# Attention and channel mix on one core: q and k turned on VectorE instead of TensorE, scores as 32-row matmuls, the mix as scaled copies and a sum

## The chip, the core and the metric

The kernel runs on one core of a Trainium2 chip. The engines are called as in the profile: PE (TensorE), DVE (VectorE), ACT (ScalarE), POOL (GpSimd, here mostly the issuer of loads) and SP (SyncE, the issuer of the other DMAs). The metric is the device time of one execution in microseconds (us).

## What is computed

Eight batches of sliding-window attention with eight heads feed a channel mix (two dense layers and a gate).

```python
def _attn_ref(q, k, v):                      # each 8 x 8 heads x 576 x 64
    scores = scale * np.matmul(q, k.transpose(0, 1, 3, 2))
    bias = slopes[:, None, None] * (-np.abs(rel).astype(np.float32))[None, :, :]
    mask = (rel >= 0) & (rel < window)       # window = 128
    scores = np.where(mask, scores + bias[None], -1000000000.0)
...
    return np.matmul(attn, v)                # attn: softmax of the scores

def _moe_ref(x, mu_k, mu_r, w_k, w_v, w_r):  # x: 8 x 576 x 512
    x_prev = np.concatenate([np.zeros((B, 1, D)), x[:, :-1, :]], axis=1)
    xk = mu_k * x + (1.0 - mu_k) * x_prev
    xr = mu_r * x + (1.0 - mu_r) * x_prev
    k = np.maximum(xk @ w_k, 0.0)
    v = k * k @ w_v
    r = 1.0 / (1.0 + np.exp(-(xr @ w_r)))
    return r * v
```

## The kernel before

**Pairs.** The attention runs in 32 pairs of heads (`it` = 4 b + g: batch b, heads 2g and 2g+1). A batch has 576 tokens: four key blocks of 128 (`NF`) and a tail of 64. Because of the window, key block u meets only the queries of blocks u and u+1, 256 columns.

**Getting q and k head by head in columns.** POOL loads q and k of half a batch, cast to bf16, into `ql` so that partition p holds tokens 4p to 4p+3 (L107); the 64 tail tokens go to `ts` (L101). For each pair DVE reorders q and k by token into `ct` (`by_token`, L126), PE turns them in eight 128x128 transposes into PSUM (`qk_transp`, L135), and ACT copies them to `qk` (`qk_copy`, L115). The tails of a batch take four PE transposes (L148) and two DVE copies (L154, L155).

**Scores and softmax.** `scores(it, e)` (L187) makes one half of a pair's scores in a PSUM buffer `sa`: matmuls of 64 rows (a head's 64 elements), head 0 on partitions 0 to 63, head 1 on 64 to 127. A pair has two halves with six matmuls each, of 256, 128 or 64 columns. There are two `sa` buffers; each half takes one. ACT does the exponential (L195) into `at`, DVE multiplies it with the mask (L200; batch 0 adds the distances on PE instead, L176), PE multiplies with v (L218, again into an `sa` buffer from batch 1 on; a column of ones gives the sum), DVE divides (L229, L230), PE transposes the result (L238) and ACT copies it to `xt` (L243).

**Mix and layers.** For each pair DVE forms `dl` = x - x_prev (L263) and then xk = dl mu_k + x_prev and xr = dl mu_r + x_prev (L270). Two batches together (P) go through the layers: `m1` (L281, xk times w_k, in column ranges of 256, 384 or 512), relu on ACT (L287), its square on DVE (L292), `m2a` and `m2` (L315, times w_v), `m3` (L300, xr times w_r), a tanh on ACT (L306) and the product on DVE (L321), which SP stores (L324).

**Order.** Every engine has a hand-written list, `ORDER`, that fixes the order of its work: `tq` the transposes of q and k, `pq` the copies to `qk`, `score`, `exp`, `mask`, `av` (attention times v), `norm`, `ot` and `xt` (transposed result and its copy), `xk`, `xr`, `m1`, `rl` (relu), `kk` (square), `m2a`, `m2`, `m3`, `rs` (tanh), `oo` (product), `lql`, `lts`, `lvs`, `lwk` (loads). A function `plan` emits the instructions in these orders. Each engine runs its list strictly from first to last. A store is issued with its product; SP has no list of its own.

Of the kernel before, what the change touches and what calls it, by code (L numbers as in the profile page):

```python
# [16 lines left out]
def kernel(  # L17
# [12 lines left out]
    nc = tc.nc  # L30
# [17 lines left out]
    NAT = 4  # L48
    NEARLY = G
    XMUL = ()  # L50
# [4 lines left out]
    csp = ctx.enter_context(tc.tile_pool(name="csp", bufs=3))  # L55
    xup = ctx.enter_context(tc.tile_pool(name="xup", bufs=3))
    mxp = ctx.enter_context(tc.tile_pool(name="mxp", bufs=2))
# [4 lines left out]
    p_tp = ctx.enter_context(tc.tile_pool(name="p_tp", bufs=1, space=bass.MemoryType.PSUM))  # L62
    p_mm = ctx.enter_context(tc.tile_pool(name="p_mm", bufs=3, space=bass.MemoryType.PSUM))
# [4 lines left out]
    ldr = cst.tile([128, 2, NHW, 2, NF * D], FP32, name="ldr")  # L68
    qk_buf = [cst.tile([128, 2, SM], BF16, name=f"qk{i}") for i in range(NBUF)]
    vs_buf = [cst.tile([128, NF, H, W], BF16, name=f"vs{i}") for i in range(NLD)]  # L70
    ql_buf = [cst.tile([128, 2, 2, H // 2, NF * D], BF16, name=f"ql{i}") for i in range(2)]
    ts_buf = [cst.tile([128, H, D], BF16, name=f"ts{i}") for i in range(NLD)]
    at_buf = [cst.tile([128, 2 * 1024 + 64], BF16, name=f"at{i}") for i in range(NAT)]

    tt_buf = [cst.tile([128, G, 3, 64], BF16, name=f"tt{i}") for i in range(2)]
    tv_buf = [cst.tile([128, H, W], BF16, name=f"tv{i}") for i in range(NLD)]
    xt_buf = [cst.tile([128, NPO, 2 + S], BF16, name=f"xt{i}") for i in range(2)]
# [22 lines left out]
    def load_tail(b, i):  # L100
        nc.gpsimd.dma_start(  # L101
            out=ts_buf[b % NLD][64 * i:64 * i + 64],
            in_=(q, k)[i][b, :, SM:S, :].rearrange("h p d -> p h d"))
# [13 lines left out]
    def cast_qk(g, i, f):  # L117
        if i == 0:
            T["cs", g] = csp.tile([128, 2, NF, 2, D], BF16, tag="ct", name="cs")
        f(T["cs", g][:, i].rearrange("p r h d -> p h r d"),  # L120
          ldr[:, i, g].rearrange("p h (r d) -> p h r d", d=D))

    def by_token(it):
        b, g = divmod(it, G)
        T["cs", it] = csp.tile([128, 2, NF, 2, D], BF16, tag="ct", name="ct")
# [18 lines left out]
    def tail_transp(b):  # L144
        ts = ts_buf[b % NLD]
# [6 lines left out]
    def tail_copy(b):  # L152
        t4 = T.pop(("tt", b))[:, 0:128 * G].rearrange("p (g t c) -> p g t c", g=G, t=2)
        nc.vector.tensor_copy(out=tt_buf[b % 2][:, :, 2], in_=t4[:, :, 0])  # L154
        nc.vector.tensor_copy(out=tt_buf[b % 2][:, :, 0], in_=t4[:, :, 1])  # L155
# [10 lines left out]
    def scores(it, e):  # L166
        early = it < NEARLY
        b, g = divmod(it, G)
        qk, tt = qk_buf[it % NBUF], tt_buf[b % 2]
# [19 lines left out]

    def at_half(it, e):  # L190
# [3 lines left out]
    def expo(it, e):  # L194
        nc.scalar.activation(out=at_half(it, e), in_=T.pop(("sa", it, e)),  # L195
                             func=AF.Exp, scale=float(scale))
# [26 lines left out]
    def norm(it, t0, t1):  # L223
# [3 lines left out]
        if t0 == 0 or it < G:  # L227
            xu = T["xu", it, t0] = xup.tile([128, NJ, 2, D], BF16, tag="xu", name="xu")
# [5 lines left out]
    def x_transp(it, t0=0, t1=NJ):  # L234
        xu = T.pop(("xu", it, t0))
        tp = T["xt", it, 128 * t0] = p_tp.tile([128, 1024], BF16, tag="tp", name="tp")
# [4 lines left out]
    def x_copy(it, c0=0, c1=S):  # L241
        b, g = divmod(it, G)
        nc.scalar.copy(out=xt_buf[b % 2][:, g, 2 + c0:2 + c1], in_=T.pop(("xt", it, c0))[:, c0:c1])  # L243

    def x_scaled(it, c0, c1):
        if c0 == 0:
            T["xm", it] = mxp.tile([128, S], BF16, tag="xm", name="xm", bufs=3)
        nc.scalar.activation(out=T["xm", it][:, c0:c1], in_=xt_buf[0][:, it, 2 + c0:2 + c1],
                             func=AF.Identity, scale=mu_sb[:, it:it + 1])

    def mix(it, which, c0=0, c1=S):
        b, g = divmod(it, G)
        P, e = divmod(b, 2)
        xc, xp = xt_buf[b % 2][:, g, 2 + c0:2 + c1], xt_buf[b % 2][:, g, 1 + c0:1 + c1]
        scaled = it in XMUL
        if which == 0:
            if e == 0 and g == 0 and c0 == 0:
                T["xk", P] = mxp.tile([128, NPO, SP], BF16, tag="xk", name="xk")
                T["xr", P] = mxp.tile([128, NPO, SP], BF16, tag="xr", name="xr")
        if c0 == 0 and which == int(scaled):  # L260
            T["dl", it] = mxp.tile([128, S], BF16, tag="dl", name="dl", bufs=4)
# [637 lines left out]
```

## Time and profile before

| | us |
|---|---|
| median of three runs (244.85 to 245.68) | 245.48 |
| span of the profiled execution, from its first to its last instruction | 243.3 |
| lies outside the span, by the median | 2.2 |
| PE busy | 232.5 |
| DVE busy | 202.5 |
| ACT busy | 173.6 |
| POOL busy | 77.2 |

The profiled execution has no time of its own beside its span; the runs' median is set against it. In the prediction, a row of the timeline gives the start, the duration, engine, source line, operation, tiles and count; neighbours of one kind are merged. The distance from one start to the next is what an instruction costs its engine in a dense stretch. A row of the groups ends with busy us, mean ns of one instruction, and the idle time before them with what ended it. A row of the stretches gives the length and then PE, PEld (weight loads), DVE, ACT and POOL busy time with counts, the granted PE clock as a share, the share in which DMA engines were busy and GB/s. The columns of the 40 slices are tenths of busy time.

### The profile page before, as it was taken

Reading aid. Unit: us, or ns where it says so; the run is one execution under the profiler, and the core shown is the slowest. Engines: PE = TensorE matmul, PEld = TensorE weight load, DVE = VectorE, ACT = ScalarE, POOL = GpSimd, SP = SyncE. Lnnn points to the kernel's source line nnn. Section 1 sums busy time; section 2 is a strip of 40 time slices with the busy share of each in tenths; the row PEclk is TensorE's granted clock in tenths of the full one; section 3 lists DMA queues with packets and bytes.
Section 4 is the critical chain, followed back from the end, with each engine's and each line's share of the span. In section 5 each row is a group of like instructions: output and inputs, shape, how many; then the busy total and the mean of one; then the engine's idle time right before and its main releaser. Section 6 shows DMA issues by size and latency. Waiting matters only on the chain.

```text
span 243.3 us, 5721 instructions
## 1 busy us (share of the span) xinstructions
PE 232.5 (96%) x2295; PEld 140.1 (58%) x2295; DVE 202.5 (83%) x448; ACT 173.6 (71%) x281; POOL 77.2 (32%) x115
## 2 busy tenths in 40 slices
PE   7499989999999999999999999999999999999993
PEld 2246776657766656557566575565565656545641
DVE  6388999999999999998989989988779876883333
ACT  6378799979999896986977768878854666307700
POOL 8999485486272825100980000000000000000000
PEclk9999999999999999999999999999999999999999
DMA  7999999999997999921999120110201300132023
GB/s 135 160 155 191 158 174 205 167 185 223 193 150 95 153 194 108 167 52 46 96 174 212 51 89 0 46 46 0 86 34 55 132 1 1 46 129 86 0 89 131
DMA packets 70748, 26.86 MB, mean 110 GB/s; under 512 B 47161, under 2 KB 66113, under 8 KB 70721
## 3 DMA queue, kind: packets, MB, share of 16 engines
q0 software_dynamic: 64976, 16.52, 77.3%
q1 hardware_dynamic: 5744, 9.97, 11.3%
q8 instruction: 18, 0.29, 0.5%
q14 instruction: 10, 0.07, 0.1%
HBM read 33.56 MB, written 9.44 MB: 177 GB/s over the span
## 4 chain that ended last, share of the span: by engine, by line
PE 85%; DVE 8%; DMA 3%; POOL 1%; issue 1%; ACT 1%; POOLq 0%; DVEq 0%
PE pv L315 26%; PE ps L281 24%; PE pr L300 13%; PE sa L187 6%; PE sa L218 6%; PE tp L135 5%; PE tp L238 4%; DMA ql<-in_k_dram 3%; DVE xu L230 2%; DVE xk L270 1%; DVE xr L270 1%; DVE ct L126 1%; DVE kk L292 1%; DVE dl L263 1%; PE to L148 1%
## 5 line engine op out<-in xcount | busy, mean ns | idle before, releaser
L195 ACT ACTIVATE at<-sa 128x1024 bf16<-128x1024 f32 x64 | 65.4, 1037 | 12.1 <-PE sa L187 11.9
L281 PE MATMUL ps<-xk,wk_sb 128*128 128x256 bf16 (+2 forms) x416 | 73.2, 314 | 0.6 <-DVE xk L270 0.6
L315 PE MATMUL pv<-wv_sb,kk 128*128 128x512 bf16 x288 | 69.4, 379 | 0.0
L287 ACT ACTIVATE rl<-ps 128x256 bf16<-128x256 f32 (+2 forms) x104 | 46.9, 475 | 20.8 <-PE ps L281 16.6
L281 PEld LDWEIGHTS <-wk_sb 128*128 128x128 bf16 x416 | 38.2, 98 | 21.5 <-issue 1.3
L292 DVE TENSOR_TENSOR kk<-rl 128x256 bf16<-128x256 bf16 (+2 forms) x104 | 32.7, 335 | 12.9 <-ACT rl L287 12.6
L315 PEld LDWEIGHTS <-kk 128*128 128x128 bf16 x288 | 26.7, 98 | 27.5 <-issue 0.8
L115 ACT COPY qk<-tp 128x1024 bf16<-128x1024 bf16 (+1 forms) x32 | 31.0, 969 | 9.1 <-PE tp L135 5.1
L200 DVE TENSOR_TENSOR at<-at,mask 128x1024 bf16<-128x1024 bf16 x56 | 37.3, 683 | 0.0
L300 PE MATMUL pr<-wr_sb,xr 128*128 128x512 bf16 x144 | 36.0, 379 | 0.0
L87 POOL DMA_DIRECT2D vs<-in_v_dram x32 | 28.5, 905 | 22.5 <-PE sa L218 18.0
L321 DVE SCALAR_TENSOR_TENSOR ot<-rs,pv 128x512 f32<-128x512 bf16 x36 | 24.6, 683 | 11.8 <-PE pv L315 11.6
L270 DVE SCALAR_TENSOR_TENSOR xk<-dl,mu_sb,xt 128x576 bf16<-128x576 bf16 (+2 forms) x36 | 27.1, 752 | 1.3
L243 ACT COPY xt<-tp 128x576 bf16<-128x576 bf16 (+2 forms) x36 | 21.3, 591 | 8.8 <-PE tp L238 8.7
L306 ACT ACTIVATE rs<-pr 128x512 bf16<-128x512 f32 x36 | 22.1, 618 | 5.6 <-PE pr L300 5.5
L270 DVE SCALAR_TENSOR_TENSOR xr<-dl,mu_sb,xt 128x576 bf16<-128x576 bf16 x32 | 25.8, 810 | 0.0
L218 PEld LDWEIGHTS <-at 128*128 128x128 bf16 x576 | 21.6, 98 | 4.7 <-ACT at L195 0.3
L230 DVE TENSOR_TENSOR xu<-sa,rc 128x640 bf16<-128x640 f32 x28 | 23.1, 824 | 1.0
L135 PE MATMUL tp<-ident,ct 128*128 128x128 bf16 x248 | 19.0, 219 | 4.0 <-DVE ct L126 4.0
L135 PEld LDWEIGHTS <-ct 128*128 128x128 bf16 x248 | 15.5, 98 | 8.7 <-DVE ct L126 5.1
L300 PEld LDWEIGHTS <-xr 128*128 128x128 bf16 x144 | 13.3, 98 | 12.1
L187 PE MATMUL sa<-qk 64*128 64x256 bf16 (+1 forms) x256 | 19.8, 259 | 0.4 <-ACT at L195 0.3
(63 smaller groups left out, 215.6 us busy)
## 6 DMA issues: line engine op xcount, KB each, us to landing
out_dram<-ot SPq DMA_DIRECT2D x36, 256.0 KB, 2.0
vs<-in_v_dram POOLq DMA_DIRECT2D x32, 128.0 KB, 7.2
ql<-in_q_dram POOLq DMA_DIRECT2D x15, 256.0 KB, 7.7
ql<-in_k_dram POOLq DMA_DIRECT2D x15, 256.0 KB, 8.2
wk_sb<-in_moe_w_k_dram POOLq DMA_DIRECT2D x2, 512.0 KB, 7.9
wv_sb<-in_moe_w_v_dram POOLq DMA_DIRECT2D x2, 512.0 KB, 10.7
ts<-in_q_dram POOLq DMA_DIRECT2D x8, 64.0 KB, 7.3
ts<-in_k_dram POOLq DMA_DIRECT2D x8, 64.0 KB, 6.3
```

Source lines behind the costliest of these rows:

```text
L115: nc.scalar.copy(out=dst, in_=src)
L135: nc.tensor.transpose(tp[:, 128 * (n - NF * t0):128 * (n - NF * t0) + 128], cs[:, n // NF, n % NF].rearrange("p h d -> p (h d)"), ident)
L187: nc.tensor.matmul(sa[:, hl, c0:c0 + n], lhsT=kk_, rhs=qq_, start=not early, stop=True, skip_group_check=True)
L195: nc.scalar.activation(out=at_half(it, e), in_=T.pop(("sa", it, e)), func=AF.Exp, scale=float(scale))
L200: nc.vector.tensor_tensor(out=at_half(it, e), in0=at_half(it, e), in1=mask[:, 2 * g:2 * g + 2, 256 * e:256 * e + 512], op=ALU.mult)
L218: nc.tensor.matmul(pa[:, hl, W * (t - t0):W * (t - t0) + W], lhsT=at[:, lo:lo + 128], rhs=vs[:, u, 2 * g + hl, :] if u < NF else tvb[:, 2 ...
L270: nc.vector.scalar_tensor_tensor(out=to, in0=T["dl", it][:, c0:c1], scalar=mu_sb[:, NPO * which + g:NPO * which + g + 1], in1=xp, op0=ALU. ...
L281: nc.tensor.matmul(ps[:, 0:c1 - c0], lhsT=wk_sb[:, po, 128 * fo:128 * fo + 128], rhs=xk[:, po, c0:c1], start=(po == 0), stop=(po == NPO - 1))
L287: nc.scalar.activation(out=rl[:, 0:c1 - c0], in_=T.pop(("ps", P, c0, fo))[:, 0:c1 - c0], func=AF.Relu, scale=RELU_SCALE)
L292: nc.vector.tensor_tensor(out=T["kk", P, c0][:, fo, 0:c1 - c0], in0=rl[:, 0:c1 - c0], in1=rl[:, 0:c1 - c0], op=ALU.mult)
L300: nc.tensor.matmul(pr, lhsT=T["xr", P][:, po, 128 * c:128 * c + 128], rhs=wr_sb[:, po], start=(po == 0), stop=(po == NPO - 1))
L315: nc.tensor.matmul(pv, lhsT=kk[:, fo, o:o + 128], rhs=wv_sb[:, fo], start=(fo == 0), stop=(fo == NFO - 1))
```

## The change

**q and k of batches 1 to 7.** They no longer go through `ct`, PE and `qk`. `turn` (L176) reads a half batch of q or k in `ql` as four-byte words, each holding two neighbouring bf16 elements, and transposes blocks of 32 partitions by 32 words on DVE. Afterwards partitions 32u to 32u+31 hold block u of 128 tokens, one word of the head on each partition and the two elements of the word beside each other. `turn_tail` (L184) does the same for the tails, on 32 partitions. `shift` (L192) is a DMA on SP within SBUF that puts the queries of block u+1 beside those of block u. Batch 0 goes the old way.

**Scores of batches 1 to 7.** `scores4` (L237, L242) makes all scores of a pair at once in both `sa` buffers: for each head and each of the two elements of a word four matmuls of 32 rows, one on each group of 32 partitions and each into its own bank, then two of 64 columns for the tail. The exponential reads them in another arrangement (L258).

**Mix.** For xk and xr each, two scaled copies (x mu and x (1 - mu), L315) and a sum with one of them shifted by a token (L317).

**Squares.** 67 of the 104 squares of the relu are done on ACT (L341).

**Buffers and orders.** The PSUM pool of the transposes goes to the pool of the layers (four buffers instead of three and one). Buffers of batch 0 lie in memory that is used later. Every list of `ORDER` is new, and SP has one, with shifts (`sh`) and stores (`st`); on POOL `lwk` stands behind the loads of batch 1's q and k.

```diff
-    p_tp = ctx.enter_context(tc.tile_pool(name="p_tp", bufs=1, space=bass.MemoryType.PSUM))
-    p_mm = ctx.enter_context(tc.tile_pool(name="p_mm", bufs=3, space=bass.MemoryType.PSUM))
+    p_mm = ctx.enter_context(tc.tile_pool(name="p_mm", bufs=4, space=bass.MemoryType.PSUM))
...
+    def turn(b, w, i):
+        hs = slice(w * H // 2, (w + 1) * H // 2)
+        dst = words(kt_buf[b % 2], 128)[:, hs] if i else words(q2_buf[b % 2], 256)[:, hs, 0:128]
+        nc.vector.transpose(
+            dst.rearrange("p h (c r) -> p h r c", r=NF),
+            ql_buf[b % 2][:, w, i].rearrange("p h c -> p (h c)").bitcast(FP32).rearrange(
+                "p (h r d) -> p h r d", r=NF, d=32))
+
+    def turn_tail(b, i):
+        dst = (words(kl_buf[b % 2], 128)[96:128, :, 0:64] if i else
+               words(q2_buf[b % 2], 256)[96:128, :, 128:192])
+        nc.vector.transpose(
+            dst.rearrange("p h (c r) -> p h r c", r=2),
+            tl_buf[b % 2][64:96, i].rearrange("p h c -> p (h c)").bitcast(FP32).rearrange(
+                "p (h r d) -> p h r d", r=2, d=32))
+
+    def shift(b, w):
+        hs = slice(w * H // 2, (w + 1) * H // 2)
+        qt = words(q2_buf[b % 2], 256)[:, hs]
+        nc.sync.dma_start(out=qt[0:96, :, 128:256], in_=qt[32:128, :, 0:128])
...
+        for hl in range(2):
+            h = 2 * g + hl
+            for par in range(2):
+                for u in range(NF):
+                    r, n = 32 * u, 256 if u < NF - 1 else 192
+                    nc.tensor.matmul(
+                        T["sa", it, u // 2][:, u % 2, 256 * hl:256 * hl + n],
+                        lhsT=kt[r:r + 32, h, :, par], rhs=qt[r:r + 32, h, 0:n, par],
+                        start=(par == 0), stop=(par == 1), skip_group_check=True)
+            for par in range(2):
+                nc.tensor.matmul(
+                    T["sa", it, 1][:, 1, 256 * hl + 192:256 * hl + 256],
+                    lhsT=kl[96:128, h, :, par], rhs=qt[96:128, h, 128:192, par],
+                    start=(par == 0), stop=(par == 1), skip_group_check=True)
...
-        if which == int(scaled):
-            nc.vector.tensor_tensor(out=T["dl", it][:, c0:c1], in0=xc, in1=xp, op=ALU.subtract)
...
-        nc.vector.scalar_tensor_tensor(
-            out=to, in0=T["dl", it][:, c0:c1],
-            scalar=mu_sb[:, NPO * which + g:NPO * which + g + 1], in1=xp, op0=ALU.mult, op1=ALU.add)
+        for i in range(2):
+            m = NPO * (2 * i + which) + g
+            nc.vector.tensor_scalar(out=mb[:, 1 - i, 2 + c0:2 + c1], in0=xc,
+                                    scalar1=mu_sb[:, m:m + 1], scalar2=None, op0=ALU.mult)
+        nc.vector.tensor_tensor(
+            out=T["xk" if which == 0 else "xr", P][:, g, S * e + c0:S * e + c1],
+            in0=mb[:, 1, 2 + c0:2 + c1], in1=mb[:, 0, 1 + c0:1 + c1], op=ALU.add)
...
+        if (P, c0, fo) in ACT_SQ:
+            nc.scalar.activation(out=out_, in_=in_, func=AF.Square)
...
-            score.5.0 tq.6 m1.0.256.4 m1.0.256.5 m1.0.256.6 av.4 score.5.1 m1.0.256.2 tail.2 ot.4
+            m1.0.256.2 m1.0.256.5 score.6 m1.0.0.7 m1.0.0.2 m1.0.256.6 m1.0.256.7
```

More of the change, by code (lines that the diff above doesn't have):

```diff
@@ L48 @@
     NAT = 4
+    NMB = 4
     NEARLY = G
-    XMUL = ()
     NHW = 1
@@ L242, in x_copy @@
         b, g = divmod(it, G)
[L243 to L249, printed above, removed]
+        nc.scalar.copy(out=xt_buf[b % 2][:, g, c0:c1], in_=T.pop(("xt", it, c0))[:, c0:c1])
     def mix(it, which, c0=0, c1=S):
@@ L514, in add_pair @@
         else:
+            war = ([("score", G * (b - 2) + i) for i in range(G)] if b > 2 else
+                   [("score", i, h) for i in range(G) for h in range(2)] if b == 2 else [])
             if g == 0:
[L516 to L519 removed]
```

477 lines of the change are left out of this document (260 added, 217 removed).

## The prediction

> **What bounds the kernel now.** I read the page's busy shares first, then its 40 slices, then the chain that ended last.
>
> ```profile
> span 243.3 us, 5721 instructions
> ...
> PE 232.5 (96%) x2295; PEld 140.1 (58%) x2295; DVE 202.5 (83%) x448; ACT 173.6 (71%) x281; POOL 77.2 (32%) x115
> ```
> ```profile
> PE   7499989999999999999999999999999999999993
> ...
> PE 85%; DVE 8%; DMA 3%; POOL 1%; issue 1%; ACT 1%; POOLq 0%; DVEq 0%
> ```
>
> PE is busy for 96% of the span, has a 9 in every slice from the eighth to the last but one, and makes up 85% of the chain; DVE's 83% over the whole span may hide a stretch in which it is full too, which is looked at below. The busy number can't price PE's work, since the ends of matmuls are modelled and overlap. I price by distances between starts, from one stretch of PE's timeline:
>
> ```profile
> 100.21 0.44 PE L238 MATMUL tp<-ident,xu 128*128 128x128 bf16 x5
> 100.58 0.34 PE L187 MATMUL sa<-qk 64*128 64x256 bf16 x4
> ...
> 100.82 0.38 PE L187 MATMUL sa<-qk 64*128 64x256 bf16 x4
> 101.13 1.04 PE L281 MATMUL ps<-xk,wk_sb 128*128 128x512 bf16 x4
> 102.00 0.61 PE L135 MATMUL tp<-ident,ct 128*128 128x128 bf16 x8
> 102.45 0.81 PE L300 MATMUL pr<-wr_sb,xr 128*128 128x512 bf16 x3
> ```
>
> Start to start, five transposes and the gap behind them take 0.37 us, and 5 of 56 ns are 0.28: the remaining 0.09 is lost on going into the 64-row score matmuls. The scores of one pair take 100.58 to 101.13, 0.55, of which 0.1 is lost on going out and 0.44 is streaming (0.22 of the last 0.31 for two pairs of 256 columns, 0.11 a pair: the two heads of a pair stream beside each other). The eight q/k transposes take 102.00 to 102.45, 0.45. For the long matmuls the end of the chain gives the price:
>
> ```profile
> 224.95 0.33 PE ps L281 x2
> ...
> 229.17 1.75 PE ps L281 x16
> 230.92 8.65 PE pv L315 x40
> ```
>
> 40 matmuls of 512 columns in 8.65 us: 216 ns each; in the same way 256 columns cost 109 ns (16 in 1.75) and 384 columns 163. The 18 matmuls that multiply attention with v cost 0.54 us a pair before and after.
>
> As a test of these prices I multiplied them with the counts in the hand-written PE order of before: 219.0 us of work, plus 39 entries into score matmuls (31 of them from batch 1 on) at 0.19 us for both switches, is 226.4. The last matmul group ends at 230.92+8.65 = 239.57, so 13.1 us of the span are PE idle, and busy times by stretches say where:
>
> ```profile
> 0.00:40.00 40.00, 32.99 (x395) 21.38 (x396) 31.99 (x96) 29.60 (x53) 32.99 (x59) 1.00 1.70 166
> 40.00:60.00 20.00, 20.00 (x231) 12.25 (x230) 19.72 (x41) 17.31 (x26) 12.46 (x17) 1.00 2.04 193
> 60.00:80.00 20.00, 20.00 (x233) 13.48 (x230) 19.39 (x44) 19.39 (x33) 9.57 (x13) 1.00 1.40 143
> 80.00:100.00 20.00, 20.00 (x219) 11.59 (x217) 19.72 (x42) 16.69 (x24) 10.82 (x14) 1.00 1.44 158
> ```
>
> After 40 us PE (the first busy column) loses nothing, at a granted clock of 1.00; DVE (the third) has 1.2 us free in 60. The 7.0 us free in the first 40, and some waits there that the modelled ends hide, are the 13.1. So PE work taken out after 40 us shortens the run one for one, as long as DVE can follow. That "as long as" is the prediction.
>
> **The change part by part.**
>
> *PE.* Batches 1 to 7 have 28 pairs. Each loses 8 transposes (0.45 us) and a quarter of the four tail transposes of its batch (0.06). The scores become 20 matmuls of 32 rows: per head two passes (even and odd elements of the bf16 pairs) of 256, 256, 256 and 192 columns, one on each group of 32 partitions and each into its own PSUM bank, and two of 64. If the four groups stream beside each other, as the two heads do now, each group carries 512 columns per head, 213 ns, and with starts 3 to 4 ns apart a pair takes 0.46 us against 0.44. Entries fall from 39 to 36. The order of after then sums to 205.3+6.8 = 212.1 us: 14.3 less.
>
> Two things here are shown by no row. Both operands are now read with a step of two elements: a set of four matmuls that streams at half rate takes 0.11 us longer, and a pair has four, so between 0 and 0.44 us a pair, 0 and 12 us in all. And there are four row groups instead of two: between full overlap and none, which is 16 matmuls of 0.1 us and four of 0.03 instead of 0.46, +1.3 us a pair, 36 in all. I take full rate and full overlap, since the nearest rows, with two groups, show both. A gain below 0.44 us is excluded, as each group has the 512 columns per head that it has now.
>
> *DVE.* The prices, again start to start:
>
> ```profile
> 36.96 0.81 DVE L270 SCALAR_TENSOR_TENSOR xr<-dl,mu_sb,xt 128x576 bf16<-128x576 bf16 x1
> 37.69 1.29 DVE L200 TENSOR_TENSOR at<-at,mask 128x1024 bf16<-128x1024 bf16 x2
> 38.89 0.28 DVE L292 TENSOR_TENSOR kk<-rl 128x256 bf16<-128x256 bf16 x1
> 39.10 0.28 DVE L154 COPY tt<-to 128x256 bf16<-128x256 bf16 x1
> ...
> 39.49 0.67 DVE L126 COPY ct<-ql 128x1024 bf16<-128x1024 bf16 x1
> ...
> 41.47 0.45 DVE L263 TENSOR_TENSOR dl<-xt 128x576 bf16<-128x576 bf16 x1
> 41.95 0.82 DVE L270 SCALAR_TENSOR_TENSOR xk<-dl,mu_sb,xt 128x576 bf16<-128x576 bf16 x1
> 42.69 0.69 DVE L200 TENSOR_TENSOR at<-at,mask 128x1024 bf16<-128x1024 bf16 x1
> ...
> 44.09 0.42 DVE L126 COPY ct<-ql 128x1024 bf16<-128x1024 bf16 x1
> 44.43 0.49 DVE L292 TENSOR_TENSOR kk<-rl 128x256 bf16<-128x256 bf16 x2
> ```
>
> xr 0.73, one mask 0.60, the tail copies 0.39, dl and xk together 1.22, ct 0.34, one square of 256 columns 0.20. The duration of a row is 0.08 more than its distance to the next, because neighbours overlap.
>
> ```profile
> L321 DVE SCALAR_TENSOR_TENSOR ot<-rs,pv 128x512 f32<-128x512 bf16 x36 | 24.6, 683 | 11.8 <-PE pv L315 11.6
> ...
> L292 DVE TENSOR_TENSOR kk<-rl 128x384 bf16<-128x384 bf16 x32 | 10.7, 351 | 5.7 <-ACT rl L287 5.6
> ...
> L112 DVE COPY qk<-tp 128x512 bf16<-128x512 bf16 x4 | 2.7, 686 | 1.4 <-PE tp L135 0.7 <-ACT qk L115 0.7
> ...
> L361 DVE TENSOR_SCALAR sid<-ident 128x128 bf16<-128x128 bf16 x8 | 1.2, 264 | 0.0
> ...
> L372 DVE COPY mask<-mask 128x2048 bf16<-128x2048 bf16 x1 | 0.7, 686 | 0.0
> ...
> L372 DVE COPY mask<-mask 128x1536 bf16<-128x1536 bf16 x1 | 0.6, 550 | 0.0
> ```
>
> Gone: 28 ct (9.4 us), seven times two tail copies (2.8), and 67 of 104 squares, which go to ACT: 33 of 256 columns at 0.20, 20 of 384 at 0.27 (351 ns less the overlap), 14 of 512 at 0.335 by the same slope, 16.7 in all.
>
> Added: 28 turns of 128 partitions x 512 words of four bytes, and 14 tail turns of 32 x 512. No row is a turn. The lower bound is the rate of a copy in SBUF (L372: 136 ns for 512 more elements), 0.2 us. L321 and L112 move 512 elements one by one in 683 and 686 ns, 0.60 start to start. The upper bound is twice their 0.53 of streaming, 1.13. I take 0.60: a turn moves one word at a time too, and it writes with a step (16 bytes) as L112 does (8 bytes), which costs L112 nothing against L321. 42 x 0.60 = 25.2 us; the bounds give 8 and 47.
>
> Mix: two scaled copies and a sum in place of a difference and a multiply-add. The slope of L372 gives a copy of 576 elements 0.15+0.07 = 0.22 us, and L361 shows that multiplying by a scalar is no slower than copying (eight in 1.2 us). The sum costs what dl costs (0.45, or 0.37 to the next). The second copy waits as dl does, whose successor starts 0.03 after its end instead of 0.08 before: 0.33. So 0.92 for one mix, 1.84 a pair against 1.22+0.73 = 1.95, and 3.7 us less with batch 0's. Bounds: 0.81 without that wait, 1.83 with copies at the rate of xr, which would be +58 us in all and counts with the slow turns below.
>
> By the counts of before's order DVE has 198.0 us of work; 198.0 - 9.4 - 2.8 - 16.7 - 3.7 + 25.2 = 190.6. But the turns all lie early and many squares that left lay late. Counted along the orders of before, DVE has 165.8 us to do up to the last mask of pair 29, and PE 179.8 up to the matmuls with v of that pair; of after, 169.3 and 166.2. So DVE goes from 14 us ahead of PE to 3 us behind it.
>
> DVE's order in before, up to the masks of pair 10 (ct is q and k by token, ql what was loaded, at the probabilities):
>
> ```order
> L126 COPY ct<-ql_94 128x1024
> L270 SCALAR_TENSOR_TENSOR xr<-dl,mu_sb,xt_108 128x576
> L292 TENSOR_TENSOR kk<-rl 128x384
> L126 COPY ct<-ql_94 128x1024 x2
> L200 TENSOR_TENSOR at_100<-at_100,mask 128x2x512 x2
> ```
>
> In after, ahead of the first mask of the same pair (kt and qt are turned k and q, kl the tails, mb the scaled copies):
>
> ```order
> L176 STREAM_TRANSPOSE kt_86<-ql_80 128x4x4x32
> L176 STREAM_TRANSPOSE qt_90<-ql_80 128x4x4x32
> L184 STREAM_TRANSPOSE qt_90<-kl_88 32x8x2x32
> L315 TENSOR_SCALAR mb_100<-xt_94,mu_sb 128x576 x2
> L317 TENSOR_TENSOR xk_97<-mb_100 128x576
> L262 TENSOR_TENSOR at_83<-at_83,mask 128x2x512
> ```
>
> Three copies of 0.34 have become three turns of 0.60 in front of a mask for which PE's matmuls with v wait.
>
> *ACT.* It loses 28 copies of 0.89 us (41.66 to 42.55 below), 25.0, and gains 67 squares. No row squares on ACT; the relu rows bound them (0.28 to 0.49 start to start), and I take 0.29, 0.40 and 0.505: 24.6 us.
>
> ```profile
> 41.66 1.02 ACT L115 COPY qk<-tp 128x1024 bf16<-128x1024 bf16 x1
> 42.55 0.42 ACT L287 ACTIVATE rl<-ps 128x256 bf16<-128x256 f32 x1
> ```
>
> ACT keeps 159 us of work by its order, 53 less than PE. Before, around the exponentials of pair 10 (at):
>
> ```order
> L287 ACTIVATE rl<-ps 128x256
> L195 ACTIVATE at_99<-sa 128x2x512
> L115 COPY qk_88<-tp 128x1024
> L287 ACTIVATE rl<-ps 128x256 x2
> L195 ACTIVATE at_100<-sa 128x2x512 x2
> ```
>
> In after, up to the same exponentials:
>
> ```order
> L341 ACTIVATE kk<-rl 128x384
> L341 ACTIVATE kk<-rl 128x256
> L334 ACTIVATE rl<-ps 128x256 x2
> L304 COPY xt_94<-xp 128x576
> L334 ACTIVATE rl<-ps 128x256
> L258 ACTIVATE at_83<-sa 128x2x2x256 x2
> ```
>
> Squares, each a few instructions behind its relu, stand where the copies of q and k stood; nothing new waits for another engine there.
>
> *SP and POOL.* 14 shifts (a DMA that moves turned q by 32 partitions) stand among the stores on SP, each behind its turn.
>
> ```profile
> out_dram<-ot SPq DMA_DIRECT2D x36, 256.0 KB, 2.0
> ...
> wk_sb<-in_moe_w_k_dram POOLq DMA_DIRECT2D x2, 512.0 KB, 7.9
> ```
> ```profile
> 13.14 0.85 POOL L375 DMA_DIRECT2D wk_sb<-in_moe_w_k_dram  x1
> ```
> ```profile
> 23.86 0.49 PE L281 MATMUL ps<-xk,wk_sb 128*128 128x256 bf16 x3
> ```
>
> A store lands in 2.0 us. The turns stand ten or more DVE instructions (5 us) ahead of the masks of their pairs, so a shift of the same kind is hidden and I cost it at nothing; where that cover is gone, a shift costs up to its 2 us, and the stores queued behind it on SP wait too, which nobody waits for until the end. On POOL the load of wk moves behind seven memsets and some four loads of 0.85 us more, by an estimate 5 us: 18.1, and with 7.9 to landing 26.0. PE reaches its first use after 16.1 us of work (14.0 before) and the 9.9 us idle that 23.86 now leaves: 26.0. So the shift of wk costs nothing, and up to the 2 us of an error in either.
>
> *Sum.* By PE: 212.1 + 13.1 idle + 3.7 from the last matmul to the end of the span = 228.9. By DVE: the dl at 41.47 has 31.4 us of DVE work ahead of it by the order, so DVE is 10.1 us behind its own sum there; with the 1.2 of the next 60 us, the mask of pair 29 ends at 169.3 + 11.3 = 180.6; PE then has 45.9 us left, and 0.3 to start, 45.9 and 3.7 make 230.5. Outside the span lie 245.48 - 243.3 = 2.2 us, by the median of the runs. So 231.1 by PE and 232.7 by DVE; the later one holds: **233**.
>
> **The rivals.**
>
> *Tail turns empty the pipe* (13%). They read partitions 64 to 95 and write 96 to 127, between neighbours that start at 0. If the 0.08 us of overlap is lost on going in and out, 28 x 0.08 = 2.3 us on DVE: 235. The Trainium skill (VectorE: DVE Perf Modes, Two Vector instructions with no wait between them) says that an instruction whose start quadrant differs is held until all earlier ones have finished; this trace has no such neighbours.
>
> *Scores at half rate* (11%). PE +12 us: 231.1+12 = 243. For it speaks that no row reads with a step, against it nothing but the rows with none.
>
> *A new wait* (10%). Both PSUM buffers of the scores must now be free at once, where before each half took one. If each pair waits 0.28 us, as PE's scores once do in the ramp (below), 28 x 0.28 = 7.8: 241.
>
> ```profile
> 35.29 0.34 PE L187 MATMUL sa<-qk 64*128 64x256 bf16 x4 [0.28 <-ACT at L195]
> ```
>
> For it: DVE is late by then, and the buffer is freed by its reciprocals; against it: PE has other matmuls between.
>
> *Slower: turns at two cycles a word* (14%). Every word of a turn goes 16 bytes behind the last one. If DVE pays a cycle for that, 42 x 0.53 = 22 us come on top, all 42 ahead of pair 29's masks and with 1.2 us in 60 free to hide them: 233+22 = 255. It decides from (245.5-233)/42 = 0.30 us more, that is 0.90 a turn. Against it: L112's 8 bytes cost nothing. The Trainium skill (SBUF — State Buffer, the note on cachelines) says that SBUF has 16-byte lines and that an access that goes to a new line pays; by that rule a turn pays with each word, the scores' step of 4 bytes doesn't, and the time would be this rival's. No run here shows it yet.
>
> *Slower still: no overlap of the row groups* (3%). 231+36 = 267; here the change doesn't do what it says.
>
> **How the numbers follow.** The forecast, both engines near full and neither rival in force, has 49%. Its own spread is 229 (mix without the wait, PE bounds) to 237; the likeliest time is 233. With emptied pipe, half rate and new wait that makes 83%, less some 3% whose edge lies near 245. The range 228 to 244 reaches to these and leaves out both slower rivals (17%). Since 0.3% is about what a measurement of this kernel can tell from no change: faster 0.80, same 0.03, slower 0.17.
>
> **What would show it.** Turn rows of 0.68 us mean, copies of the mix of 0.30 and sums of 0.45; the scores of a pair in 0.65 us from the last neighbour's end to the next one's start; DVE full until pair 29 and PE waiting in small pieces for masks and norms, 1 to 4 us in all after 40 us. The prediction is wrong if a turn takes over 0.9 us, if the scores of a pair take over 1 us, or if PE waits over 5 us after 40 us.

## The result, and the profile after

The changed kernel takes **258.2 us** (median of 4 runs, 256.7 to 262.2), before beside it 245.6 (244.9 to 246.2): 1.050 times as long, 95% interval 1.046 to 1.054. Forecast were 233, and 228 to 244 as the range: the sign is wrong. The execution that was profiled is the 262.2, at a mean granted clock of 0.961; the other three took 256.7 to 258.3 at 0.972 to 0.980, so its span is some 4 us too long.

The page of after, in the order in which before was read:

```profile
span 260.4 us, 5725 instructions
...
PE 227.3 (87%) x2234; PEld 133.7 (51%) x2267; DVE 215.7 (83%) x481; ACT 171.9 (66%) x320; POOL 76.6 (29%) x118
...
PE   8794539997849989898899889998989999999993
...
DVE  6688299999996999999999999999999976465232
...
PEclk9889577999988999999999999999999999999999
...
DVE 45%; PE 34%; DMA 11%; issue 5%; ACT 2%; POOL 0%; DVEq 0%; POOLq 0%; ACTq 0%
PE ps L328 11%; DVE at L262 9%; DVE mb L315 9%; PE pv L365 9%; DMA qt<-qt 9%; PE pr L350 6%; DVE xu L291 5%; DVE ot L371 5%; DVE qt L176 4%; DVE kt L176 3%; DMA ql<-in_k_dram 3%; DVE xr L317 3%; DVE xk L317 2%; PE sa L237 2%; PE sa L280 2%
```

PE has given up its place in the chain: 34% where it had 85%. DVE has a 9 in every slice but one from the sixth to the 32nd (208 us), and 45% of the chain. And there is an entry that before did not have: 9% of the span is spent on shifts (qt<-qt). The stretches (busy us of PE, PEld, DVE, ACT and POOL, then the granted clock) say the same:

```profile
0.00:40.00 40.00, 26.59 (x281) 15.56 (x283) 28.05 (x83) 21.65 (x37) 31.50 (x60) 0.81 1.47 165
...
60.00:80.00 20.00, 14.70 (x173) 9.41 (x177) 19.59 (x38) 12.21 (x24) 8.93 (x13) 0.91 1.13 158
...
100.00:200.00 100.00, 91.94 (x992) 53.41 (x1000) 98.00 (x206) 74.95 (x127) 20.39 (x26) 1.00 0.67 102
200.00:260.00 60.00, 56.20 (x373) 31.02 (x378) 33.30 (x82) 29.03 (x63) 0.00 (x0) 1.00 0.16 62
```

PE loses 13.4 us in the first 40 (before 7.0) and 5.3 between 60 and 80, at a clock that has fallen to 0.81 and 0.91. From 100 to 200 us DVE is busy for 98.0 of 100 us and PE for 91.9. Behind 200 us PE is full again. What DVE does in that time, by groups (busy us and mean ns behind the bar):

```profile
L315 DVE TENSOR_SCALAR mb<-xt,mu_sb 128x576 bf16<-128x576 bf16 x120 | 40.7, 381 | 3.2 <-ACT xt L304 2.9
...
L176 DVE STREAM_TRANSPOSE kt<-ql 128x512 f32<-128x512 f32 x14 | 15.3, 1096 | 0.0
L176 DVE STREAM_TRANSPOSE qt<-ql 128x512 f32<-128x512 f32 x14 | 15.3, 1093 | 0.0
...
L184 DVE STREAM_TRANSPOSE qt<-kl 32x512 f32<-32x512 f32 x7 | 4.9, 705 | 0.2
```

A turn lasts 1.09 us where 0.68 were forecast, a scaled copy 0.38 where it was 0.30. Start to start, in DVE's timeline:

```profile
101.32 0.64 DVE L315 TENSOR_SCALAR mb<-xt,mu_sb 128x576 bf16<-128x576 bf16 x2
102.00 0.46 DVE L317 TENSOR_TENSOR xr<-mb 128x576 bf16<-128x576 bf16 x1
102.37 1.10 DVE L176 STREAM_TRANSPOSE kt<-ql 128x512 f32<-128x512 f32 x1
103.33 0.67 DVE L262 TENSOR_TENSOR at<-at,mask 128x1024 bf16<-128x1024 bf16 x1
104.01 0.70 DVE L184 STREAM_TRANSPOSE qt<-kl 32x512 f32<-32x512 f32 x1
104.64 0.66 DVE L184 STREAM_TRANSPOSE kl<-kl 32x512 f32<-32x512 f32 x1
105.34 1.10 DVE L176 STREAM_TRANSPOSE kt<-ql 128x512 f32<-128x512 f32 x1
106.29 0.68 DVE L262 TENSOR_TENSOR at<-at,mask 128x1024 bf16<-128x1024 bf16 x1
```

A turn takes 0.95 us, a mix 1.05 (101.32 to 102.37). The tail turns take 0.63 and 0.70, and the mask ahead of them 0.68, 0.08 more than the 0.60 of a mask otherwise.

The shift is read best in the chain, here from 18 to 40 us in order of time (start, us, what):

```profile
18.84 1.01 DVE qt L176
...
19.87 8.85 DMA qt<-qt
...
28.76 0.56 PE sa L237 x3
...
30.84 0.56 DVE xu L291
31.40 1.00 DVE qt L176
...
32.43 6.53 DMA qt<-qt
...
39.09 0.56 PE sa L237 x3
```
```profile
PE sa L237 <- DMA qt<-qt: 9.4, 3, 4.7
...
PE sa L237 <- DVE xu L291: 2.2, 3, 1.1
```

The turn, the shift, the scores, the norms and the next turn follow one upon the other, and 15.4 of these 21 us are two shifts on their way. PE's waits (us in all, times, longest) show what PE itself loses to shifts: 9.4 us, in three places. DVE stands still behind the first for 5.1 us, since the norms that it has next wait for matmuls that stand behind these scores on PE. The first 253 us of run e_prices below are the same program once more, and its last product ends 4.4 us earlier: there the first two shifts take 4.4 and 8.8 us, and PE waits 6.8 us for shifts, again in three places. Of the six other runs below that keep the shift, five have 4.3 to 5.4 for the first and 8.1 to 10.2 for the second, and one has 8.5 and 6.8. So one of the two takes over 8 us each time.

What came out as forecast is on PE. The scores of a pair, 43.74 to 44.31 here, take 0.57 us with the switch out; the way in costs 0.10 more (the two matmuls ahead of them start 0.20 apart, where 256 columns cost 0.11), so 0.67 against a forecast of 0.65. Four row groups do stream beside each other, and at full rate.

```profile
40.07 3.74 PE L328 MATMUL ps<-xk,wk_sb 128*128 128x256 bf16 x24
43.74 0.41 PE L237 MATMUL sa<-qt,kt 32*128 32x256 bf16 x8
...
44.31 0.94 PE L328 MATMUL ps<-xk,wk_sb 128*128 128x256 bf16 x7
```

### The profile page after: what moved, and what is told of

The parts are those of the page before. It is cut to its first block, busy times and chain, and to the rows that moved or that the text cites. A ratio compares the mean times of both kernels' runs of the same rounds, so it can differ in the third digit from the quotient of the medians.

```text
span 260.4 us, 5725 instructions
## 1 busy us (share of the span) xinstructions
PE 227.3 (87%) x2234; PEld 133.7 (51%) x2267; DVE 215.7 (83%) x481; ACT 171.9 (66%) x320; POOL 76.6 (29%) x118
## 4 chain that ended last, share of the span: by engine, by line
DVE 45%; PE 34%; DMA 11%; issue 5%; ACT 2%; POOL 0%; DVEq 0%; POOLq 0%; ACTq 0%
PE ps L328 11%; DVE at L262 9%; DVE mb L315 9%; PE pv L365 9%; DMA qt<-qt 9%; PE pr L350 6%; DVE xu L291 5%; DVE ot L371 5%; DVE qt L176 4%; DVE kt L176 3%; DMA ql<-in_k_dram 3%; DVE xr L317 3%; DVE xk L317 2%; PE sa L237 2%; PE sa L280 2%
## 5 line engine op out<-in xcount | busy, mean ns | idle before, releaser
L258 ACT ACTIVATE at<-sa 128x1024 bf16<-128x1024 f32 x64 | 64.3, 1028 | 27.0 <-PE sa L242 20.6
L328 PE MATMUL ps<-xk,wk_sb 128*128 128x256 bf16 (+2 forms) x412 | 74.8, 318 | 4.9 <-DVE xk L317 2.9
L365 PE MATMUL pv<-wv_sb,kk 128*128 128x512 bf16 x274 | 67.2, 379 | 1.7 <-DVE ot L371 0.8
L315 DVE TENSOR_SCALAR mb<-xt,mu_sb 128x576 bf16<-128x576 bf16 (+2 forms) x136 | 44.9, 377 | 3.2 <-ACT xt L304 2.9
L341 ACT ACTIVATE kk<-rl 128x256 bf16<-128x256 bf16 (+2 forms) x67 | 32.2, 500 | 0.2
L237 PE MATMUL sa<-qt,kt 32*128 32x256 bf16 x448 | 20.5, 275 | 12.2 <-DMA qt<-qt 9.4
L356 ACT ACTIVATE rs<-pr 128x512 bf16<-128x512 f32 x36 | 21.7, 610 | 10.6 <-PE pr L350 10.3
L304 ACT COPY xt<-xp 128x576 bf16<-128x576 bf16 (+2 forms) x36 | 20.8, 590 | 7.3 <-PE xp L299 6.8
L237 PEld LDWEIGHTS <-kt 32*128 32x128 bf16 x448 | 10.6, 94 | 22.9 <-issue 13.6
L280 PE MATMUL sa<-vs,at 128*128 128x65 bf16 x448 | 18.9, 194 | 1.3 <-DVE at L262 1.1
L343 DVE TENSOR_TENSOR kk<-rl 128x256 bf16<-128x256 bf16 (+2 forms) x37 | 12.0, 343 | 9.4 <-ACT rl L334 9.4
L120 POOL DMA_DIRECT2D ql<-in_q_dram x15 | 11.7, 781 | 22.0 <-DVE qt L176 18.7
```

The lines of the kernel that those rows point to most:

```text
L237: nc.tensor.matmul(T["sa", it, u // 2][:, u % 2, 256 * hl:256 * hl + n], lhsT=kt[r:r + 32, h, :, par], rhs=qt[r:r + 32, h, 0:n, par], star ...
L258: nc.scalar.activation(out=to, in_=sa, func=AF.Exp, scale=float(scale))
L280: nc.tensor.matmul(pa[:, hl, W * (t - t0):W * (t - t0) + W], lhsT=at[:, lo:lo + 128], rhs=vs[:, u, 2 * g + hl, :] if u < NF else tvb[:, 2 ...
L315: nc.vector.tensor_scalar(out=mb[:, 1 - i, 2 + c0:2 + c1], in0=xc, scalar1=mu_sb[:, m:m + 1], scalar2=None, op0=ALU.mult)
L328: nc.tensor.matmul(ps[:, 0:c1 - c0], lhsT=wk_sb[:, po, 128 * fo:128 * fo + 128], rhs=xk[:, po, c0:c1], start=(po == 0), stop=(po == NPO - 1))
L341: nc.scalar.activation(out=out_, in_=in_, func=AF.Square)
```

## The experiments

**Theory.** The time is the end of the last mask of pair 29 on DVE plus 50 us, as the prediction's second sum had it, and DVE gets there late for three reasons: turns at 0.95, mixes at 1.05, and shifts that take 2.7 to 8.8 us (5.0 in the middle). **Rival:** PE's waits for the shift and the low clock behind them set the time, and DVE only fills it. Further rivals: the new order in the first 40 us, or ACT with its 67 squares.

### Prices by themselves

Behind the last product of after, with no other engine at work:

```
+        for d in dst:                       # the turn as it is; further forms in the same way
+            nc.vector.transpose(d.rearrange("p (h c r) -> p h r c", h=4, r=4), tin)
+        for d in dst:
+            nc.vector.transpose(d.rearrange("p (h r c) -> p h r c", h=4, r=4), tin)
...
+                nc.vector.tensor_scalar(out=mb_buf[i % 4][:, i // 4, o:o + n], in0=x[:, 0:n],
+                                        scalar1=mu_sb[:, i:i + 1] if ptr else 0.5, ...
```

> After, with rows behind its last product that belong to no output: six forms of turn, four of each (as in the kernel, written with a step of 16 bytes; written without a step; with a step of 8 bytes; read with a step of 16 bytes and written without one; on 32 partitions without a step, in place; the same from partitions 64-95 to 96-127), five forms of scaled copy, eight of each, and four shifts one behind the other while no other transfer runs. Theory step (the 16 bytes between two words of a turn cost time): 0.945 us start to start with the step, 0.60 to 0.70 without it, 0.73 or less at 8 bytes. Theory own rate (a turn of 128 partitions costs 0.945 however it is written): the first four forms all at 0.94. For the scaled copies: 0.28 us with a scalar from memory; if that scalar costs the 0.06 us that my price lacked, 0.22 with a number in the instruction; if the offset of 4 bytes costs it, 0.22 without the offset. For the shifts: 2 to 2.5 us to landing if the 5.0 us of after come from the transfers beside them, 4 us or more if a shift takes that by itself.

DVE's timeline there. L956 is the turn as in the kernel, L958 writes without a step, L960 with one of 8 bytes, L963 reads with 16 bytes and writes without, L966 and L969 use 32 partitions; of the copies, those without mu_sb have the number in the instruction:

```profile
252.95 3.77 DVE L956 STREAM_TRANSPOSE kt<-ql 128x512 f32<-128x512 f32 x4
256.57 2.44 DVE L958 STREAM_TRANSPOSE kt<-ql 128x512 f32<-128x512 f32 x4
258.94 2.45 DVE L960 STREAM_TRANSPOSE kt<-ql 128x512 f32<-128x512 f32 x4
261.31 3.92 DVE L963 STREAM_TRANSPOSE kt<-ql 128x512 f32<-128x512 f32 x4
265.26 2.48 DVE L966 STREAM_TRANSPOSE kt<-ql 32x512 f32<-32x512 f32 x4
267.76 2.48 DVE L969 STREAM_TRANSPOSE kt<-ql 32x512 f32<-32x512 f32 x4
270.26 2.33 DVE L974 TENSOR_SCALAR mb<-xt,mu_sb 128x576 bf16<-128x576 bf16 x8
272.50 1.83 DVE L974 TENSOR_SCALAR mb<-xt 128x576 bf16<-128x576 bf16 x8
274.25 3.96 DVE L974 TENSOR_SCALAR mb<-xt,mu_sb 128x576 bf16<-128x576 bf16 x16
278.12 1.23 DVE L974 TENSOR_SCALAR mb<-xt 128x288 bf16<-128x288 bf16 x8
```

From one row's start to the next, by four: 0.90 us for a turn with its step, **0.59** without, 0.59 at 8 bytes, 0.99 (0.96 between two of a kind) when the 16 bytes are on the reading side. By eight: 0.280 for a copy with mu from memory, **0.219** with the number in the instruction. The 16 copies of the third such row are eight of 576 elements without the offset (0.279 apart) and eight of 288 (0.204); the last row's 288 with a number are 0.144 apart. So mu from memory costs 0.06 us whatever the length, and the offset costs nothing. The first of the four shifts:

```profile
qt<-qt SPq DMA_DIRECT2D x1, 192.0 KB, 2.8
```

2.8 us to landing with no load beside it, only the end of the last store just ahead, and 3.2 to 3.6 for the three behind it. In after, too, the shifts with no load at work land in 2.7 us (issued at 157.6 and 170.9), while one among loads takes 7.2 (125.8) and the first two 8.8 and 6.5. So the long ones lie among loads; that the loads make them long is likely by these rows, but no run takes the loads away from the first shifts. Even alone a shift is no store of 2.0.

### One edit undone at a time

Beside the runs from here on before itself took 244.7 to 245.8 us, so a difference between two kernels is good to about 1 us. The mix of before in after:

```
-            nc.vector.tensor_scalar(out=mb[:, 1 - i, 2 + c0:2 + c1], in0=xc,
-                                    scalar1=mu_sb[:, m:m + 1], scalar2=None, op0=ALU.mult)
...
+            nc.vector.tensor_tensor(out=dl, in0=xc, in1=xp, op=ALU.subtract)
+        nc.vector.scalar_tensor_tensor(
+            out=T["xk" if which == 0 else "xr", P][:, g, S * e + c0:S * e + c1], in0=dl,
+            scalar=mu_sb[:, NPO * which + g:NPO * which + g + 1], in1=xp, op0=ALU.mult, op1=ALU.add)
```

> After with the mix of before (a difference, then two multiply-adds, reading the padded x). Theory DVE (the time is the end of the last mask of pair 29 on DVE plus the 50 us behind it): a mix costs 0.98 us in place of 1.05, 58 of them ahead of that mask, and the 3 us by which copies were stretched go as well: 7 us less, 251 us. Theory shift (PE's waits for the shifted q set the time): 257 to 259 us, as after.

254.5 us, 1.037 times before (1.031 to 1.043): 3.7 less, about half of what DVE was to gain.

Turns without a step:

```
-            dst.rearrange("p h (c r) -> p h r c", r=NF),
+            dst.rearrange("p h (r c) -> p h r c", r=NF),
```

> After with turns that write without a step (tokens then stand in another order inside each block of 128, so that masks and v no longer fit them: the arrangement of tokens is left out, the work is the same). Theory DVE with a priced step: 28 turns at 0.60 to 0.70 us in place of 0.945, 7 to 10 us less, 249 to 251 us. Theory own rate: turns stay at 0.94 and the time at 258. Theory shift: turns get shorter, the time stays within 2 us of after.

252.9 us, 1.033 (1.030 to 1.037): 5.3 less. The step is what makes a turn long in the kernel too:

```profile
L176 DVE STREAM_TRANSPOSE kt<-ql 128x512 f32<-128x512 f32 x14 | 9.8, 701 | 0.0
```

No shifts:

```
-                op(("sh", b, w), "SP", 60, lambda: shift(b, w), ...
-            ready = [("tr", b, g // 2, 1), ("sh", b, g // 2), ("tl", b, 0), ("tl", b, 1)]
+            ready = [("tr", b, g // 2, 1), ("tr", b, g // 2, 0), ("tl", b, 0), ("tl", b, 1)]
```

> After with all 14 shifts left out (the scores of a block with the block behind it read what lies there: this part of the computation is left out) and a memset of one buffer at the start. Theory DVE: only DVE's own 5.1 us of idleness behind PE's first wait can go, 253 to 255 us. Theory shift: PE's 9.4 us of waits go and the clock no longer falls behind them, 245 to 249 us.

253.2 us, 1.034 (1.031 to 1.037): 5.0 less, the figure of the theory that has DVE as the bound; the rival's 245 to 249 is out. But together the three would give only 244, and the mix and the step fall short of what DVE has less to do.

### All three, and one put back

The three edits above in one kernel:

> All three edits at once: the mix of before, turns written without a step, no shifts (the shift and the arrangement of tokens are left out). If these three are the whole of my error, DVE up to the last mask of pair 29 is my forecast's 169.3 us, plus 58 mixes at 0.98 in place of 0.92 (3.4) and 1.8 for the tail turns, plus the 11.3 idle of before: 186, and with the 50 us behind it and 2.2 outside the span 238 us, no more than 5 above the forecast. If the gains of the single edits only add up (4, 5.5 and 5 us from 258): 243 to 244. If something else of the change costs time (the new order in the first 40 us, squares on ACT, the scores): 247 us or more.

**238.2 us**, 0.972 times before (0.964 to 0.980). Together the edits bring 20.0 us where singly they bring 14.0, and the time is what the ledger of the prediction gives with the rows put right (worked out below). So nothing else is needed to explain the miss: had the order of the first 40 us, the squares on ACT or the scores cost the time instead, 247 or more was expected of this run.

```profile
PE 222.6 (94%) x2267; PEld 130.3 (55%) x2267; DVE 201.2 (85%) x382; ACT 171.2 (73%) x320; POOL 76.3 (32%) x116
...
DVE  7889999999999999999999999999988882655132
...
PE 55%; DVE 34%; ACT 5%; issue 5%; POOL 0%; DVEq 0%; POOLq 0%
```

DVE is full here too, up to 170 us.

The step alone, put back into it:

```
-            dst.rearrange("p h (r c) -> p h r c", r=NF),
+            dst.rearrange("p h (c r) -> p h r c", r=NF),
```

> The run with all three edits, but with turns written with their step of 16 bytes again (mix of before, no shifts; the shift is left out): what the step alone costs. By the row, 28 turns take 0.945 us in place of 0.60 to 0.63, 9 to 9.7 us more on DVE, all ahead of the last mask of pair 29. If DVE is the bound at 238 us already, that counts in full: 247 to 248 us. If it is worth what it was as a single edit: 243 to 244 us. If PE was the bound at 238, most of it is hidden: 241 us or less.

247.1 us, 1.009 (1.006 to 1.012): 8.9 more, the full count of 28 turns at 0.31 to 0.35. The shift alone, put back into it:

```
+                op(("sh", b, w), "SP", 60, lambda: shift(b, w), ...
-            ready = [("tr", b, g // 2, 1), ("tr", b, g // 2, 0), ("tl", b, 0), ("tl", b, 1)]
+            ready = [("tr", b, g // 2, 1), ("sh", b, g // 2), ("tl", b, 0), ("tl", b, 1)]
```

> The run with all three edits, but with the shifts back (the arrangement of tokens is left out): what a shift costs when DVE is no longer overloaded. If PE's 9.4 us of waits for shifts then count in full, 246 to 248 us; if a shift is worth the 5 us that leaving it out of after brought, 243 us; if it is hidden as my prediction costed it, 238 to 239 us.

248.5 us, 1.014 (1.007 to 1.021): 10.3 more. Of this PE's own waits for shifts are 4.8 us by the profile; DVE stands idle for 18.0 us up to the last mask of pair 29, without shifts 7.7, and 8.3 us of the difference stand ahead of masks, whose exponentials come out of scores that wait.

```profile
PE sa L237 <- DMA qt<-qt: 4.8, 3, 3.5
```

The landing is not all of it. The stretch from 30 to 40 us, with the shift and then without it:

```profile
30.00:40.00 10.00, 6.52 (x47) 4.38 (x45) 7.55 (x14) 5.28 (x13) 6.55 (x9) 0.50 1.52 188
```
```profile
30.00:40.00 10.00, 9.62 (x128) 7.38 (x121) 9.81 (x18) 9.93 (x26) 7.14 (x9) 0.93 1.58 187
```

With the shift the granted clock is 0.5 for 10.2 us from 29.8 on and for 3.4 us near 71; without it, for 3.4 us once. The 24 matmuls of m1 behind the second shift's scores take 5.2 us there and 3.4 here. So the 10.3 us hold both the waits and slower matmuls behind them, by an estimate from these figures 4.8 us and at most 5.1 (half of 10.2); no run takes the two apart.

Why single edits fall short is seen here: while DVE waits for what the shift holds up, shorter instructions gain nothing, and while DVE is late with its own work, an earlier shift gains nothing. For seven of these kernels, in the profiled execution of each, and for after once more from the run of the prices:

| kernel | last mask of pair 29 ends | DVE idle up to there | from there to the end of the span |
|---|---|---|---|
| after | 210.0 | 18.0 | 50.4 |
| after, in run e_prices | 205.7 | 12.4 | (other work follows) |
| mix of before | 202.1 | 15.7 | 50.4 |
| turns without a step | 197.9 | 13.8 | 50.4 |
| no shifts | 200.8 | 7.9 | 50.3 |
| all three | 185.7 | 7.7 | 50.3 |
| all three but the step | 194.2 | 7.0 | 50.3 |
| all three but the shift | 195.7 | 18.0 | 50.4 |

The last column doesn't move. In these seven kernels the time is the end of that mask plus 50.3 us (49.9 in the prediction), and DVE's work and idleness ahead of it are the whole difference. Single edits are better set beside the second row, since the first holds the 4 us named with the result: without shifts the mask ends 4.9 us earlier than in the second row, where the medians differ by 5.0, and with DVE's own work shortened by the mix or the step its idle time there is not shorter (15.7 and 13.8, against 12.4).

### Ways around it that did not work

Half of each mix on ACT, so that DVE has 20 us less to do:

```
+                nc.scalar.mul(to, xc, mu_sb[:, m:m + 1])
...
+                nc.vector.scalar_tensor_tensor(out=to, in0=xp, scalar=mu_sb[:, m:m + 1],
+                                               in1=to, op0=ALU.mult, op1=ALU.add)
```

> After with half of each mix on ACT for batches 1 to 7: ACT writes x times mu where the mix belongs, DVE adds the shifted x times (1 - mu) in one multiply-add. The same result is computed. Theory DVE: 0.73 us in place of 1.05 for 56 mixes, and no stretched copies, 20 us less on DVE; PE with its 212 us of work, 13 of early idleness, the 9 it waits for shifts and 3.7 behind it becomes the bound: 238 to 242 us, faster than before. Rival theory ACT: 56 more instructions of 0.55 us put ACT at 203 us of 240, exponentials queue behind them and PE waits for these: 246 us or more.

268.5 us, 1.092 (1.083 to 1.101): the rival on ACT holds. The 56 scaled copies add 37 us to ACT (0.66 each, 0.55 expected), and ACT is busy for 76 of the 80 us from 80 to 160, with the exponentials queued in it:

```profile
PE 231.3 (86%) x2267; PEld 134.1 (50%) x2267; DVE 198.4 (74%) x353; ACT 209.1 (77%) x376; POOL 76.2 (28%) x116
...
ACT  6383649995959899999899987997979469854820
```

The scores of pairs 4 and 5 behind the first matmuls of the channel mix, as in before:

```
-            av.1.1 score.4 av.2.1 ot.0.1 av.3.1 ot.2.1 ot.1.1 score.5 ot.3.1 m1a.0.0.0
-            m1.0.0.0 m1a.0.0.1 m1.0.0.1 score.7 ...
+            av.1.1 av.2.1 ot.0.1 av.3.1 ot.2.1 ot.1.1 ot.3.1 m1a.0.0.0
+            m1.0.0.0 m1a.0.0.1 m1.0.0.1 score.4 score.5 score.7 ...
```

> After with the scores of pairs 4 and 5 behind the first two output groups of the first matmul of the channel mix on PE, as they stood in before, and their exponentials moved with them on ACT; nothing else. Theory order: PE's 4.7 us of waiting for the first shift is filled with work that was ready at 27 us, the last norms of batch 0 no longer stand behind it, and DVE's 5.1 us of idleness goes: 252 to 254 us. Theory transfer: the wait only moves to the next place where PE needs the shift (pairs 4 and 5 still start after 33 us), DVE is no earlier with their masks: 256 to 259 us.

259.0 us, 1.054 (1.045 to 1.063), as after. PE waits for shifts only 3.0 us in place of 9.4 (6.8 in run e_prices), and it gains nothing: DVE now stands still for 3.4 us ahead of the first masks instead. So another order alone doesn't help; the second shift takes 10.2 us here, which points to the landing. With both edits:

> The last two edits together. If DVE is the bound that the first removes, the second counts in full on PE: 3 to 5 us below the half mix on ACT alone, 234 to 238 us. If both take the same idleness away, within 1.5 us of it.

269.9 us, 1.098 (1.088 to 1.108), no better than the half mix on ACT alone.

The shift as three copies on ACT, with the mix of before:

```
-        nc.sync.dma_start(out=qt[0:96, :, 128:256], in_=qt[32:128, :, 0:128])
+        for r in range(0, 96, 32):
+            nc.scalar.copy(out=qt[r:r + 32, :, 128:256], in_=qt[r + 32:r + 64, :, 0:128])
```

> After with the mix of before and each shift as three copies of 32 partitions on ACT in place of a transfer; the same result is computed. Three copies of 512 words at 0.6 us are 1.8 us to the last one in place of 3 to 9 to landing. If the landing time is what the shift costs: 5 us less than with the mix of before alone (254.5), 249 to 250 us. If ACT pays for 42 more copies (25 us on an engine with 82 us free, but ahead of exponentials, as the half mix on ACT did): 254 us or more.

253.6 us, 1.038 (1.028 to 1.048), against 254.5 with the transfer: nothing that the intervals would tell apart. And with turns without a step, the line of that edit, as well:

> The same with turns written without a step as well (the arrangement of tokens is left out). If ACT's copies hide: 238 to 240 us, as without any shift. If they cost as a transfer does: 243 to 247 us. It is the time that a version could reach whose masks and v follow the tokens' new order.

252.9 us, 1.032 (1.025 to 1.039), 14.7 above the run without any shift and 4.4 above the transfer. The copies cost what the groups say, 25.9 us on ACT, and they stand ahead of exponentials.

```profile
L193 ACT COPY qt<-qt 32x512 f32<-32x512 f32 x42 | 25.9, 616 | 3.4 <-DVE qt L176 2.7
```

So no version that computes everything beat before. The 238.2 is what the change would be worth with turns that need no step and q that needs no shift. The step could go if masks, v and the transposes of x followed another order of tokens inside each block of 128; that wasn't tried, since by the run with the shift put back it would end near 248.5.

## Why the prediction was wrong, point by point

**The frame was right.** PE's ledger, "as long as DVE can follow", and the sum by DVE over the last mask of pair 29 hold. With the three prices put right the same sum gives, for the kernel without step and shift and with the mix of before, 169.3 us, plus 58 mixes at 0.98 in place of 0.92 (3.4), plus 1.8 for the tail turns, plus 11.3 and 49.9 and 2.2: 237.9, and 238.2 was measured. That the two agree to 0.3 us is partly luck: the 11.3 that DVE is behind its own sum is carried over from before, where it was counted from starts, while that run's trace shows 7.7 us of idle time. Scores (0.67 us a pair with both switches) came out as forecast, and so did squares on ACT (0.31, 0.41 and 0.52 us start to start against 0.29, 0.40 and 0.505) and the load of wk (without shifts the first matmul with it starts at 27.2, forecast 26.0); the new wait on sa is 2.2 us in all, far below that rival's 7.8.

**The step that failed first: the turn at 0.60.** The prediction held that a turn "writes with a step (16 bytes) as L112 does (8 bytes), which costs L112 nothing against L321". The 8 bytes do cost nothing, for a turn either (0.59), and 0.60 was right for a turn without a step. The fault was to carry 8 over to 16. A turn with 16 costs 0.95: +0.35 on 28 turns, 8.9 us by the run that puts only the step back. The rival "turns at two cycles a word" named the place and the point from which it decides (0.90); its price of 0.53 was too high, and it doesn't hold for the tail turns, whose step is 8 bytes. The Trainium skill (SBUF — State Buffer, the note on cachelines) says that an access which goes to a new 16-byte line pays unless at least two accesses fall on a line: 4-byte words at 8 bytes do, at 16 they don't, and the prices 0.59 and 0.90 agree. The prediction quoted this rule and gave its rival 14%, because a row with half the step showed no cost; by that rule such a row is no evidence.

**The second: the shift at nothing.** "A store lands in 2.0 us" was the wrong neighbour. A store runs late, among little else; the first shifts run at 20 and 32 us, among the loads of two batches, and took 8.8 and 6.5 us in the profiled execution, and 4.3 to 5.4 and 8.1 to 10.2 in six of the seven other runs with a shift. Even alone a shift takes 2.8. The prediction gave it a cover of 5 us and "up to its 2 us" if that was gone. What it missed is the landing of the second and what waits behind it: the next norms and the next turn, as the chain from 18 to 40 us shows, and PE's matmuls at half the granted clock. 7.4 us by the run of the mix of before against that with no shifts as well (254.5 and 247.1), 10.3 when nothing else holds DVE up, of which the waits and the clock are not taken apart.

**The third, smaller: the mix at 0.92.** "L361 shows that multiplying by a scalar is no slower than copying" holds for a number in the instruction (0.219 against a forecast of 0.22); mu is read from memory, and that costs 0.06 a copy. A mix is 1.05, more than before's 0.98, where 0.06 less was forecast: 3.7 us.

The three, taken away one behind the other, are 3.7, 7.4 and 8.9: the 20.0 us between 258.2 and 238.2. How they divide depends on the order, as the table shows; the sum doesn't.

**The chances.** DVE was put 3 us behind PE at the last mask of pair 29, so every error in a DVE price counted in full; "faster: 0.80" fitted a sum with slack on both engines, not one in which 42 instructions that no row showed stood in front of the end. The tail turns did empty the pipe (the 13% rival), for some 2 us.

## What to carry to other kernels

When a change moves work onto an engine that will then be the bound, price its new instructions from both ends and let the upper end into the forecast: the nearest row has to share the property that may cost (here the step in bytes, and where a scalar comes from), not only the element count. A transfer between two dependent steps is priced by its landing at the time of day at which it runs, with the loads beside it, and by all that stands behind its waiter on the other engines. When single undoings fall short, undo all together: causes that hide each other add up only then.

## What the runs showed of the hardware that was not expected

A turn on 32 partitions takes as long as one on 128 (0.59 between two of a kind). The 16 bytes cost about as much on the reading side (0.96) as on the writing side (0.90 to 0.95).

Scaled copies are stretched when POOL issues a DMA. Here two copies take 1.03 us to the start of their sum, in place of the 0.68 above, and POOL issues at that time:

```profile
112.90 0.99 DVE L315 TENSOR_SCALAR mb<-xt,mu_sb 128x576 bf16<-128x576 bf16 x2
113.93 0.46 DVE L317 TENSOR_TENSOR xk<-mb 128x576 bf16<-128x576 bf16 x1
```
```profile
112.97 0.79 POOL L120 DMA_DIRECT2D ql<-in_k_dram  x1
113.71 1.82 POOL L95 DMA_DIRECT2D vs<-in_v_dram  x2
```

Ten of the 120 copies of 576 elements last 0.1 us or more longer than the middle one's 0.364, 2.4 us in all, and all ten lie beside an issue on POOL: they begin 0.2 us or more after its start and end 0.11 to 0.14 us after its end. Copies that begin in the first 0.2 us of an issue keep their length. No sum, mask or square differs from the middle one of its like by 0.02. The Trainium skill (SBUF — State Buffer, SBUF: two separate sides) says that POOL and DVE share a pair of ports, that a DVE instruction in a mode with both ports needs it, and that the one that comes first holds it to its end. The ten copies agree; the mix of before has no such instruction, since both of its kinds read two tensors.
